# Attention with a feed-forward layer on one core: exponentials as the stationary operand of AV, two-bank QK units, and full tiles throughout

## The chip, the cores and the metric

The kernel runs on 1 core of one Trainium2 chip. The metric is the device time in microseconds (us) of one execution. Each time below is the median of several executions of the same kernel; where there was one execution only, the text says so. The profile is a recording of one such execution. Its engines are PE (matmuls), PEld (loading of the stationary operand, which may overlap PE), DVE (vector), ACT (activation functions), POOL and SP. PEclk is the clock that PE was granted, as a share of full speed.

## The reference

There are eight sequences (`t`) of 576 tokens with eight heads of 64. Attention has a bias that depends on the distance of the two tokens. Its output, 4608 tokens of 512, goes through a layer with a sine in it (called MoE in the code).

```python
scores = scale * np.matmul(q, k.transpose(0, 1, 3, 2)) + bias_table[bucket(|i - j|)]   # 8 x 8 x 576 x 576
attn = np.exp(scores - scores.max(-1)); attn = attn / attn.sum(-1)
x = np.matmul(attn, v)             # -> (4608, 512)
# ... 
h = x @ w_in                       # (4608, 2048)
s = np.sin(alpha * h)
g = h + s * s / (alpha + 1e-09)
out = g @ w_out                    # (4608, 512)
```

## The kernel before

The kernel makes a plan of tasks in advance and then writes out the instructions of each engine in the planned order. An engine carries out its instructions in that order. The waits between engines are not written by hand: the framework in which the kernel is written places them, from the tiles that each instruction reads and writes.

Heads are taken in pairs (`p`). The kernel computes transposed scores: keys lie on the partitions, queries along the row. A QK unit fills one bank of PSUM (the memory into which PE writes its results), ACT takes the exponential out of the bank into `u` (float16), and DVE multiplies the entries near the diagonal by the exponential of the bias (the band). AV then streams `u` past V as the weight, and once more past a block of ones, which gives the sum of each row in all 64 partitions of a head. The division is done as exp(-ln(sum)) on ACT and a multiplication on DVE.

```python
NBUF = {"sc": 4, "av": 2, "mo": 2, ...}        # PSUM: 8 banks of 128 x 512 float32

def new_sc():                                  # one score bank, four in rotation
    return ps.tile([128, 512], F32, name="sc", tag="sc", bufs=NBUF["sc"])

def mm2(out, lhsT, rhs, start, stop):          # two matmuls of 64 columns side by side
    for z in range(2):
        nc.tensor.matmul(out=out[64*z : 64*z+64], lhsT=lhsT[:, 64*z : 64*z+64], rhs=rhs, ...)

# a QK unit and its exponential: one bank (14 units per head pair)
def qk(e, ...):
    sc.v = new_sc()
    for y in range(nc_):
        for g in range(2):
            nc.tensor.matmul(out=sc.v[64*g : 64*g+64, n*y : n*y+n], lhsT=kzs[t%2][:, p, k0 : k0+64],
                             rhs=qTs[t%2][:, p, q0 : q0+n], start=True, stop=True)
def ex(e, ...):
    nc.scalar.activation(out=u.v[:, k0 : k0+nc_, q0 : q0+n], in_=sc.v[:, 0 : n*nc_], func=AF.Exp, scale=0.125)

# AV for a window of n queries (384, then 192): y = 0 gives the sums, y = 1 the values
def mm(e, y=y):
    o = avs[y].v = new_av()
    mm2(o[:, 0:n], (vhs[t%2][:, p] if y else ones2)..., u.v[:, 8, q0 : q0+n], True, False)
    for c in range(4):
        for z in range(2):
            nc.tensor.matmul(out=o[64*z : 64*z+64, 0:n],
                             lhsT=vs[t%2][:, c, 2*p+z, :] if y else ones,
                             rhs=u.v[:, 4*z+c, q0 : q0+n], ...)
# ACT: ln = Ln(sums); rd = Exp(-ln).   DVE: xT[:, p, ...] = avs[1] * rd
# ... 
# MoE-in for 512 tokens, f = 0..15; it uses the same four score banks
h.v = new_sc()
for j in range(4):
    mm2(h.v, w_in16[:, j, 128*f : 128*f+128], xT[:, j, ...512], j == 0, j == 3)
s16 = Sin(alpha * h)        # ACT
sq = s16 * s16              # ACT or DVE
g[:, f] = sq * inv_a + h    # DVE, reads h from the score bank again
# ... 
# MoE-out: 36 groups of 16 matmul pairs in the "mo" banks, used as filling for PE
```

In the steady part MoE-out of the previous tokens fills the gaps of PE during attention. ACT changes its function table twice per `t`, which marks the two phases in the trace: from the table of Exp to that of Sin is attention, from Sin to Exp is MoE-in.

The softmax here doesn't subtract the row's maximum and nothing guards it: scores larger than these inputs give would overflow.

## Time and profile before

The time is 446.31 us (three runs, 445.49 to 446.52).

| | before |
|---|---|
| span of the profiled run | 444.2 us |
| PE busy | 423.1 us, 95% |
| ACT busy | 382.9 us, 86% |
| second table load (end of the attention of t=0) | 50.0 us |
| attention + MoE-in, each t | 28.9 + 17.1 us |

The first fence is taken from the page of before: the busy time of each engine with the number of its instructions, and the busy tenths of PE and ACT and the granted clock in 40 equal slices.

```profile
span 444.2 us, 12031 instructions
PE 423.1 (95%) x4934; PEld 306.1 (69%) x4934; DVE 262.4 (59%) x554; ACT 382.9 (86%) x834; POOL 84.5 (19%) x95
...
PE   5579999999999999999999999999999999999996
...
ACT  3459999999999999999999999999999999946511
...
PEclk8659999999999999999999999999999999999999
```

From the fourth slice on PE is at 9 tenths or more at full clock, and so is ACT until the tail. A full PE with a full ACT beside it means that a gain has to come from PE, and that the plan has little slack.

The next fence has the groups of before that the change touches: instruction, its operands and count, then busy time and mean time of one, then how long the engine had been idle before them and what ended most of that.

```profile
L565 ACT ACTIVATE u<-sc 128x384 f16<-128x384 f32 x448 | 175.3, 527 | 7.6 <-PE sc L557 7.4
L377 PE MATMUL mo<-w_out,g 128*64 128x512 f16 x1152 | 172.2, 379 | 0.0
L557 PE MATMUL sc<-qT,kz 128*64 128x192 f16 (+1 forms) x1152 | 134.8, 296 | 8.8 <-DVE qT L470 5.3
L377 PE MATMUL sc<-xT,w_in 128*64 128x512 f16 x1152 | 132.7, 379 | 1.3 <-DVE g L708 1.3
```

The idle columns of the PE groups are what to read: 8.8 and 1.3 us in the whole run. PE hardly ever waits for a score bank. The mean time of a matmul (379 ns for 512 columns) holds its way through the array; what a matmul costs in a stream is the distance between two starts, which the timeline gives as 216 ns.

The view of the waits says the same for the stretch from 60 to 370 us. These are all its lines for PE: who waited for whom, total us, how often, and the longest.

```profile
PE sc L557 <- ACT u L565: 2.1, 5, 0.6
PE sc L377 <- DVE g L708: 0.5, 1, 0.5
```

The last view of before is one row of a table by stretches: length, busy us of each engine with its number of instructions, then granted clock, DMA share and GB/s.

```profile
core 0: us, PE busy (x) PEld busy (x) DVE busy (x) ACT busy (x) POOL busy (x), PEclk, DMA share, GB/s
...
144.00:188.00 44.00, 43.61 (x522) 32.62 (x520) 28.44 (x61) 43.03 (x97) 8.79 (x8) 1.00 0.91 107
```

### The profile page before, as it was taken

Reading aid. Unit: us, or ns where it says so; the run is one execution under the profiler, and the core shown is the slowest. Engines: PE = TensorE matmul, PEld = TensorE weight load, DVE = VectorE, ACT = ScalarE, POOL = GpSimd, SP = SyncE. Lnnn points to the kernel's source line nnn. Section 1 sums busy time; section 2 is a strip of 40 time slices with the busy share of each in tenths; the row PEclk is TensorE's granted clock in tenths of the full one; section 3 lists DMA queues with packets and bytes.
Section 4 is the critical chain, followed back from the end, with each engine's and each line's share of the span. In section 5 each row is a group of like instructions: output and inputs, shape, how many; then the busy total and the mean of one; then the engine's idle time right before and its main releaser. Section 6 shows DMA issues by size and latency. Waiting matters only on the chain.

```text
span 444.2 us, 12031 instructions
## 1 busy us (share of the span) xinstructions
PE 423.1 (95%) x4934; PEld 306.1 (69%) x4934; DVE 262.4 (59%) x554; ACT 382.9 (86%) x834; POOL 84.5 (19%) x95
## 2 busy tenths in 40 slices
PE   5579999999999999999999999999999999999996
PEld 3356657876688668865886688657876787666663
DVE  4447695549654865576456755685568545927400
ACT  3459999999999999999999999999999999946511
POOL 3792931016000700080008000400000000000000
PEclk8659999999999999999999999999999999999999
DMA  9999999939900996199209960980000000011111
GB/s 193 181 206 144 163 163 147 194 81 181 110 25 26 106 146 143 42 147 168 39 27 98 156 140 1 160 104 25 27 26 0 27 26 25 2 49 47 49 72 71
DMA packets 136118, 41.51 MB, mean 93 GB/s; under 512 B 122520, under 2 KB 130768, under 8 KB 136064
## 3 DMA queue, kind: packets, MB, share of 16 engines
q0 software_dynamic: 89392, 17.67, 47.3%
q1 hardware_dynamic: 46400, 22.79, 23.4%
q8 instruction: 38, 0.62, 0.6%
q10 hardware_dynamic: 272, 0.30, 0.2%
q14 instruction: 16, 0.13, 0.1%
HBM read 37.56 MB, written 16.52 MB: 122 GB/s over the span
## 4 chain that ended last, share of the span: by engine, by line
PE 71%; ACT 16%; issue 3%; DVE 3%; DMA 3%; POOL 2%; ACTq 0%; DVEq 0%; POOLq 0%
PE mo L377 24%; PE sc L377 18%; PE sc L557 14%; PE av L631 12%; ACT s L694 6%; ACT u L565 4%; PE av L377 3%; ACT L756 2%; ACT sq L701 2%; DVE g L708 1%; DMA w_out<-e_dram 1%; DMA tabL<-in_bias_table_dram 1%; DVE kz L470 1%; ACT rd L651 1%; ACT lnd L647 1%
## 5 line engine op out<-in xcount | busy, mean ns | idle before, releaser
L565 ACT ACTIVATE u<-sc 128x384 f16<-128x384 f32 x448 | 175.3, 527 | 7.6 <-PE sc L557 7.4
L377 PE MATMUL mo<-w_out,g 128*64 128x512 f16 x1152 | 172.2, 379 | 0.0
L557 PE MATMUL sc<-qT,kz 128*64 128x192 f16 (+1 forms) x1152 | 134.8, 296 | 8.8 <-DVE qT L470 5.3
L377 PE MATMUL sc<-xT,w_in 128*64 128x512 f16 x1152 | 132.7, 379 | 1.3 <-DVE g L708 1.3
L598 DVE TENSOR_TENSOR u<-u,m 128x512 f16<-128x512 f16 (+1 forms) x192 | 73.5, 400 | 72.1 <-ACT u L565 68.6
L557 PEld LDWEIGHTS <-kz 128*64 128x64 f16 x1152 | 84.7, 112 | 42.8 <-issue 10.6
L708 DVE SCALAR_TENSOR_TENSOR g<-sq,inv_a,sc 128x512 f16<-128x512 f16 x144 | 102.0, 745 | 20.6 <-PE mo L377 10.7
L377 PEld LDWEIGHTS <-w_in 128*64 128x64 f16 x1152 | 80.3, 110 | 44.1 <-issue 2.8
L694 ACT ACTIVATE s<-sc,alphaT 128x512 f16<-128x512 f32 x144 | 92.5, 678 | 3.5 <-PE sc L377 2.5
L377 PEld LDWEIGHTS <-g 128*64 128x64 f16 x1152 | 79.1, 110 | 22.5
L329 POOL DMA_DIRECT2D v<-in_v_dram x24 | 22.3, 1065 | 176.3 <-PE av L631 176.3
L701 ACT ACTIVATE sq<-s 128x512 f16<-128x512 f16 x75 | 47.2, 629 | 2.3
L662 DVE TENSOR_TENSOR xT<-av,rd 128x384 f16<-128x384 f32 (+1 forms) x68 | 29.4, 437 | 32.9 <-ACT rd L651 24.8
L631 PE MATMUL av<-u,ones 128*64 128x192 f16 (+1 forms) x512 | 44.8, 291 | 0.0
L631 PE MATMUL av<-u,v 128*64 128x192 f16 (+1 forms) x512 | 44.7, 291 | 0.0
L703 DVE TENSOR_TENSOR sq<-s 128x512 f16<-128x512 f16 x69 | 28.9, 420 | 11.4 <-ACT s L694 11.1
L647 ACT ACTIVATE lnd<-av 128x384 f32<-128x384 f32 x64 | 28.9, 451 | 7.3 <-PE av L631 6.5
L468 ACT ACTIVATE outs<-mo 128x512 f32<-128x512 f32 x15 | 8.9, 595 | 29.3 <-PE mo L377 29.3
L631 PEld LDWEIGHTS <-ones 128*64 128x64 f16 x512 | 30.8, 112 | 5.0
L631 PEld LDWEIGHTS <-v 128*64 128x64 f16 x512 | 30.7, 112 | 3.9
L651 ACT ACTIVATE rd<-lnd 128x384 f32<-128x384 f32 x64 | 28.7, 449 | 1.4
L377 PE MATMUL av<-u,ones 128*64 128x192 f16 (+1 forms) x128 | 20.5, 291 | 2.7 <-DVE u L581 2.7
(59 smaller groups left out, 194.0 us busy)
## 6 DMA issues: line engine op xcount, KB each, us to landing
out_dram<-outs SPq DMA_DIRECT2D x36, 256.0 KB, 2.0
staged_k<-in_k_dram POOLq DMA_DIRECT2D x6, 576.0 KB, 13.6
staged_q<-in_q_dram POOLq DMA_DIRECT2D x6, 576.0 KB, 16.7
kz<-kraw SPq DMA_DIRECT2D x12, 288.0 KB, 6.3
v<-in_v_dram POOLq DMA_DIRECT2D x24, 128.0 KB, 5.4
w_out<-in_v_dram SPq DMA_DIRECT2D x8, 256.0 KB, 5.4
w_in<-in_moe_w_in_dram POOLq DMA_DIRECT2D x4, 512.0 KB, 8.8
w_out<-in_moe_w_out_dram POOLq DMA_DIRECT2D x4, 512.0 KB, 8.8
```

The lines of the kernel that those rows point to most:

```text
L377: nc.tensor.matmul(out=out[64 * z : 64 * z + 64], lhsT=lhsT[:, 64 * z : 64 * z + 64], rhs=rhs, start=start, stop=stop,)
L557: nc.tensor.matmul(out=sc.v[64 * g : 64 * g + 64, n * y : n * y + n], lhsT=kzs[t % 2][:, p, k0 : k0 + 64], rhs=qTs[t % 2][:, p, q0 : q0 + ...
L565: nc.scalar.activation(out=u.v[:, k0 : k0 + nc_, q0 : q0 + n], in_=sc.v[:, 0 : n * nc_], func=AF.Exp, scale=0.125,)
L598: nc.vector.tensor_tensor(out=io, in0=io, in1=m2[:, 2 * p : 2 * p + 2, x0 : x0 + hi - lo], op=ALU.mult,)
L631: nc.tensor.matmul(out=o[64 * z : 64 * z + 64, 0:n], lhsT=vs[t % 2][:, c, 2 * p + z, :] if y else ones, rhs=u.v[:, 4 * z + c, q0 : q0 + n] ...
L647: nc.scalar.activation(out=ln.v[:, 0:n], in_=avs[0].v[:, 0:n], func=AF.Ln)
L651: nc.scalar.activation(out=rd.v[:, 0:n], in_=ln.v[:, 0:n], func=AF.Exp, scale=-1.0)
L662: nc.vector.tensor_tensor(out=xT[:, p, (x0 + a) % XN : (x0 + a) % XN + m - a], in0=avs[1].v[:, a:m], in1=rd.v[:, a:m], op=ALU.mult,)
L694: nc.scalar.activation(out=s16.v, in_=h.v, func=AF.Sin, scale=alphaT[:, f : f + 1])
L701: nc.scalar.activation(out=sq.v, in_=s16.v, func=AF.Square)
L703: k_of(e).tensor_tensor(out=sq.v, in0=s16.v, in1=s16.v, op=ALU.mult)
L708: nc.vector.scalar_tensor_tensor(out=gcell[b].v[:, f, :], in0=sq.v, scalar=inv_a[:, f : f + 1], in1=h.v, op0=ALU.mult, op1=ALU.add,)
```

## The change

The intent is to take streaming time from PE and work from ACT.

- In AV, `u` becomes the stationary operand: 128 queries by 128 keys is a weight, and V with a column of ones (65 columns) streams past it. The sums come out as one column beside the values, so the second pass over `u` goes. The output has queries on the partitions; it is normalised per row (reciprocal and multiply on DVE), turned by a transpose on PE and copied to `xT`. Ln and Exp(-Ln) on ACT go.
- QK fills two banks at a time, and one exponential of up to 768 columns reads both: 7 in place of 14 for each head pair.
- All matmuls use the whole array (128 columns of weights) instead of two halves.
- The bands read a reversed table with a negative step, so that the table no longer has to be turned on POOL. Loads and copies at the start are reordered.

```diff
-    def new_sc():
-        return ps.tile([128, 512], F32, name="sc", tag="sc", bufs=NBUF["sc"])
+    scb = ps.tile([128, 4, 512], F32, name="sc")
+    banks = [0]
+
+    def new_sc(n):
+        b = banks[0] % 4
+        banks[0] += n
+        return scb[:, b : b + n, :] if n > 1 else scb[:, b, :]
 ...
+    m2 = m2r[:, :, ::-1]
 ...
-    def mm2(out, lhsT, rhs, start, stop):
+    def full(out, lhsT, rhs, start, stop):
+        nc.tensor.matmul(out=out, lhsT=lhsT, rhs=rhs, start=start, stop=stop)
 ...
+                sc.v = new_sc(2)
+                for z in range(2):
+                        full(sc.v[:, z, n * y : n * y + n], kz[:, p, k0 : k0 + 128],
+                             qT[:, p, q0 : q0 + n], True, True)
 ...
+                    o, x = uz[:, :, c, 0:384], sc.v[:, :, 0:384]
+                nc.scalar.activation(out=o, in_=x, func=AF.Exp, scale=0.125)
 ... (AV: for each group of 128 queries at qc)
+                full(av.v[:, x0 : x0 + 2 * VC], u.v[:, 8, qc : qc + 128], vhs[t % 2][:, p, :],
+                     True, False)
+                for z in range(2):
+                    for c in range(4):
+                        full(av.v[:, x0 + VC * z : x0 + VC * z + VC],
+                             u.v[:, 4 * z + c, qc : qc + 128], vs[t % 2][:, c, 2 * p + z, :],
+                             False, z == 1 and c == 3)
 ...
+            nc.vector.reciprocal(out=r, in_=a[:, :, :, D])
+            nc.vector.tensor_tensor(out=xn..., in0=a[:, :, :, 0:D], in1=r..., op=ALU.mult)
 ...
+                nc.tensor.transpose(out=tr.v[:, qc - q0 : qc - q0 + 128], in_=xn.v[:, i], identity=id_sb)
 ...
-            def lg(e): ... func=AF.Ln
-            def rc(e): ... func=AF.Exp, scale=-1.0
```

## The prediction

> **What bounds the kernel now.** By the page's busy table PE is busy 95% of 444.2 us and ACT 86%; the slices show both at 9 tenths from about 45 us to 395 us. Table loads cut the span into iterations of 45.9 us (attention 28.9, MoE-in about 17). By the timeline, pairs of 64-column matmuls start every 216 ns for N=512, 162 ns for N=384 and 82 ns for N=192. Per iteration that makes 13.8 (MoE-in) + 13.8 (MoE-out) + 8.8 (QK) + 9.8 (AV with ones) = 46.2 us: PE streams without gaps and is the bound, with MoE-out filling the attention phase. ACT is nearly as full (about 45 us). The first 50 us (attention of t=0) are different: PE has only about 20 us of work there, much of it at half clock, and waits for loads, band tables and exponentials. After 373 us PE works alone.
>
> **What changes.**
> 1. AV per head pair: 20 paired streams (2.45 us) become 5 groups of one N=130 and eight N=65 matmuls, with u as a 128-column weight, plus 5 transposes of N=128. The question is whether a 128-column weight load hides behind 27 ns of streaming. The Trainium skill (TensorE: Matmul & The Clock Gate, Weight-path perf modes) says that fast weight load is on for 128 weights that are not fp32. The trace agrees as far as it goes: the first transposes (128-column weight, N=96) start every 42 ns at full clock, which is their streaming time; below 42 ns nothing is shown. My estimate is 31 ns per N=65: 5 x (8 x 31 + 57) + 5 x 56 = 1.8 us, so 0.65 us saved per pair, 2.6 us per iteration. At 42 ns almost nothing would be left (2.25 us).
> 2. QK, MoE-in and MoE-out as full tiles: a pair already streams as fast as one matmul, so no PE time is saved; only half the instructions go.
> 3. ACT loses Ln and Exp(-Ln) (1.41 us per pair from start to start, 45 us in all), and 14 exponentials become 7 (51 ns fixed each, 11 us in all); it gains some 30 copies to xT (about 11 us). Net about -45 us, but PE is the bound, so this is mostly off the critical path except in t=0.
> 4. DVE: the normalising multiply stays (reciprocal added, about 0.15 us), copies to xT are added, about +25 us in all. It was 59% busy: no bound. Bands now read a reversed table; the skill (Vector Engine (DVE) Microarchitecture Reference, Performance modes) lists steps of +-1 as fit for the two-per-cycle mode, so I expect the 128x512 band to stay near 0.44 us; no trace here shows it yet.
> 5. POOL loses the four table reversals (about 0.8 us each) and copies; the first pairs no longer wait for them. With shorter ACT work, t=0 attention should end near 42 us rather than 50.
>
> **Sum.** t=1..7: 7 x 2.6 = 18 us, all on the PE-bound path; start: about 8 us. 446.3 - 26 = **420 us**, range 407 to 435. Faster by over 2%: 0.88; within 2%: 0.10; slower: 0.02.
>
> **What would show it.** N=65 matmuls start every 29 to 34 ns; iterations shrink to 43 us or so; ACT falls to about 335 us busy with gaps in attention; DVE rises to about 290; PE without idle in t=1..7; second table load near 42 us.
>
> **What would make it wrong.** Weight loads of 128 columns that do not hide (42 ns or more per N=65); only two QK units in flight (two banks each of four), so that PE waits in order for ACT; the longer chain AV, reciprocal, multiply, transpose, copy delaying MoE-in beyond what MoE-out can fill; bands falling to one element per cycle; start-up loads arriving no earlier than before.

## The result, and the profile after

The changed kernel is correct and takes 827.11 us (four runs, 825.65 to 828.23) against 446.41 us of before in the same rounds. All four runs are alike, with a mean granted clock of 0.743 to 0.757. The ratio is 1.853, with a 95% interval of 1.850 to 1.856.

The page of after, the same lines as above:

```profile
span 823.8 us, 8773 instructions
PE 545.9 (66%) x3518; PEld 255.2 (31%) x3518; DVE 302.2 (37%) x683; ACT 357.1 (43%) x502; POOL 77.9 (9%) x88
...
PE   4665577656775678556765677557855777555588
...
ACT  2663256424642356225642365226542465222231
...
PEclk9995599857985599658975599559985699555569
```

No engine is full. The instructions went as intended (8773 in place of 12031) and so did ACT's work, yet PE is busy 66% and the clock falls to half over and over. Where every engine is idle a good part of the time, the engines wait for each other. The groups show between whom:

```profile
L391 PE MATMUL sc<-xT,w_in 128*128 128x512 f16 x576 | 238.0, 561 | 181.9 <-DVE g L716 130.9
L702 ACT ACTIVATE s<-sc,alphaT 128x512 f16<-128x512 f32 x144 | 98.9, 687 | 305.3 <-PE sc L391 183.0
...
L582 ACT ACTIVATE u<-sc 128x768 f16<-128x768 f32 (+1 forms) x224 | 171.0, 786 | 119.2 <-PE sc L391 112.4
...
L391 PE MATMUL sc<-qT,kz 128*128 128x192 f16 (+1 forms) x512 | 90.7, 293 | 60.3 <-ACT u L582 47.2
```

PE stood 181.9 us before MoE-in matmuls, against 1.3 us before the change; ACT stood 305.3 us before the sine, and what ended that was mostly PE. That is a ring: PE waits for the readers of the banks, and these wait for PE. The view of the waits has one line that betrays more:

```profile
PE sc L391 <- DVE g L716: 136.6, 69, 2.7
ACT s L702 <- DVE g L716: 122.4, 64, 2.5
...
PE sc L391 <- ACT u L582: 70.6, 115, 1.6
...
PE sc L391 <- ACT s L702: 53.6, 66, 1.7
```

The second line: ACT's sine waits for DVE's `g`, 122.4 us in all. Both only read the bank, and the `g` in question belongs to another `f`, in another bank. No data passes from one to the other. The chain of waits of after, between 253 and 261 us (start, length, what), shows a full turn:

```profile
253.62 1.88 PE sc L391 x4
...
255.51 0.69 ACT s L702
...
256.25 1.88 PE sc L391 x4
...
258.21 0.76 DVE g L716
...
258.99 0.70 ACT s L702
...
259.71 0.76 DVE g L716
...
260.51 1.88 PE sc L391 x4
```

For two `f` there are two matmul groups, two sines and two `g`, strictly one after the other: 6.9 us. PE's part is 3.76 us of that, and at half clock at that: each matmul of 512 columns takes 427 ns here and 216 ns in before. Attention has the same picture. This is the timeline of after (start, length, instructions, and in brackets the idle time before and what ended it):

```profile
292.80 0.81 ACT L582 ACTIVATE u<-sc 128x768 f16<-128x768 f32 x1 [0.57 <-PE sc L391]
...
293.66 0.48 PE L391 MATMUL sc<-qT,kz 128*128 128x384 f16 x2 [0.47 <-ACT u L582]
...
294.18 0.81 ACT L582 ACTIVATE u<-sc 128x768 f16<-128x768 f32 x1 [0.57 <-PE sc L391]
...
295.04 0.40 PE L391 MATMUL sc<-qT,kt 128*128 128x288 f16 x2 [0.68 <-ACT u L582]
```

QK starts 0.05 us after the exponential has ended (292.80 + 0.81 = 293.61), the exponential after QK has ended. There are four banks and a unit needs two, yet one unit is in flight. The row by stretches that answers to the one shown of before:

```profile
144.00:188.00 44.00, 25.90 (x92) 9.02 (x90) 12.91 (x24) 14.84 (x22) 9.23 (x8) 0.65 1.01 89
```

One t now takes about 91 us (36.9 to 39.8 of attention and some 52 of MoE-in), against 46.

### The profile page after: what moved, and what is told of

The parts are those of the page before. It is cut to its first block, busy times and chain, and to the rows that moved or that the text cites. A ratio compares the mean times of both kernels' runs of the same rounds, so it can differ in the third digit from the quotient of the medians.

```text
span 823.8 us, 8773 instructions
## 1 busy us (share of the span) xinstructions
PE 545.9 (66%) x3518; PEld 255.2 (31%) x3518; DVE 302.2 (37%) x683; ACT 357.1 (43%) x502; POOL 77.9 (9%) x88
## 4 chain that ended last, share of the span: by engine, by line
PE 54%; ACT 27%; DVE 14%; issue 3%; DMA 1%; DVEq 0%; ACTq 0%
PE sc L391 40%; ACT u L582 15%; DVE g L716 12%; ACT s L702 12%; PE mo L391 9%; PE av L391 4%; DMA e_dram<-e_sb 1%; DMA phi_sb<-phi_const 1%; DVE xn L653 1%; PE av L663 0%; DVE kt L518 0%; DVE rd L652 0%; DVEq L716 0%; DVE kz L472 0%; DVE qT L472 0%
## 5 line engine op out<-in xcount | busy, mean ns | idle before, releaser
L391 PE MATMUL sc<-xT,w_in 128*128 128x512 f16 x576 | 238.0, 561 | 181.9 <-DVE g L716 130.9
L702 ACT ACTIVATE s<-sc,alphaT 128x512 f16<-128x512 f32 x144 | 98.9, 687 | 305.3 <-PE sc L391 183.0
L582 ACT ACTIVATE u<-sc 128x768 f16<-128x768 f32 (+1 forms) x224 | 171.0, 786 | 119.2 <-PE sc L391 112.4
L391 PEld LDWEIGHTS <-w_in 128*128 128x128 f16 x576 | 72.9, 127 | 338.3 <-issue 325.0
L391 PE MATMUL mo<-w_out,g 128*128 128x512 f16 x576 | 175.2, 415 | 0.0
L391 PE MATMUL sc<-qT,kz 128*128 128x192 f16 (+1 forms) x512 | 90.7, 293 | 60.3 <-ACT u L582 47.2
L610 DVE TENSOR_TENSOR u<-u,m2r 128x512 f16<-128x512 f16 (+1 forms) x192 | 72.0, 390 | 42.7 <-ACT u L582 39.9
L391 PEld LDWEIGHTS <-g 128*128 128x128 f16 x576 | 60.2, 105 | 59.9 <-issue 24.3
L391 PEld LDWEIGHTS <-kz 128*128 128x128 f16 x512 | 46.7, 99 | 95.1 <-issue 85.1
L391 PEld LDWEIGHTS <-u 128*128 128x128 f16 x1440 | 57.3, 98 | 8.9
L391 PE MATMUL av<-v,u 128*128 128x65 f16 x1280 | 55.6, 194 | 0.0
```

What stands on the lines that cost most here:

```text
L391: nc.tensor.matmul(out=out, lhsT=lhsT, rhs=rhs, start=start, stop=stop)
L582: nc.scalar.activation(out=o, in_=x, func=AF.Exp, scale=0.125)
L610: nc.vector.tensor_tensor(out=io, in0=io, in1=m2[:, 2 * p : 2 * p + 2, x0 : x0 + hi - lo], op=ALU.mult,)
L702: nc.scalar.activation(out=s16.v, in_=h.v, func=AF.Sin, scale=alphaT[:, f : f + 1])
```

## The experiments

**The theory.** The four score banks are one tile in the change. The framework keeps track of accesses by tile, not by bank, and so every access to a bank waits for the last access of another engine to any of the four. The built program bears this out: the QK unit that fills banks 0 and 1 waits until ACT has finished its 69th counted instruction, which is the exponential of banks 2 and 3; the exponential of banks 0 and 1 is the 68th. This is so throughout: in the program rebuilt from the kernel of after, all 135 waits of a QK unit for an exponential name one of the other two banks, and 128 of the 144 sines wait for a `g` of another bank (in e1 none does). **Rivals:** (B) the lost clock is the cause and the waits follow from it; (C) two units of two banks are too few for any hardware, however the waits are placed.

Experiments with three rounds have intervals; those with one run are meant for effects of tens of per cent.

### e1: only the waits

Nothing of the work, the banks or the order on any engine is changed. A helper tells the framework, for each access, that there is no dependency between different banks, and adds those within a bank by hand.

```diff
+    def free_banks(i, used, write):
+        # keep the waits between accesses of one bank, drop those between banks
+        for x, bx, wx in sc_log[-48:]:
+            if not (used & bx) and x.engine != i.engine:
+                tc.declare_no_dep(i, x, reason="other bank")
+        ...  # the last accesses of the same bank: tc.add_manual_dep(i, x.name, ...)
-                        full(sc.v[:, z, 0:288], ...)
+                        free_banks(full(sc.v[:, z, 0:288], ...), {min(sc.b) + z}, True)
```

> The changed kernel with every instruction and its order on each engine kept; only the waits between accesses of DIFFERENT banks of the one four-bank score tile are dropped (waits between accesses of one bank are declared by hand). Theory A (because the four score banks are one tile, each access waits for the last access of any of the four banks, so one unit is in flight instead of two and four): 405 to 435 us, granted clock back to about 0.97, attention about 27 us and MoE-in about 17 us per iteration. Rival B (the low clock is the cause: full tiles, N=65 matmuls or transposes do not keep the clock granted, waits are its result): clock stays near 0.75 and the time above 650 us. Rival C (what my prediction named: two units in flight are too few for ACT and PE): attention stays near 37 us, the time above 520 us.

Measured: 425.22 us (424.84 to 425.53), ratio to before 0.953 [0.951, 0.955], 25.9 + 18.1 us for each t, correct; no race was found in the built program. The same stretch, then the timeline of e1 at the start of an attention phase:

```profile
144.00:188.00 44.00, 44.00 (x407) 25.39 (x404) 32.15 (x77) 39.21 (x58) 9.24 (x8) 1.00 0.98 107
```

```profile
293.30 3.74 ACT L609 ACTIVATE u<-sc 128x768 f16<-128x768 f32 x5
```

PE is busy 44.00 of 44 us at full clock, and five exponentials run without a gap where after had about 0.57 us before each. The order of the instructions is the same as in after on every engine, so the waits alone account for 827.1 - 425.2 = 402 us. Rival C falls: two units of two banks are enough. Rival B falls as the first cause: the clock came back without being touched.

### e2: the same one line in the kernel before

If the tile is the cause, it must ruin the kernel before as well, with none of the rest of the change.

```diff
     def new_sc():
-        return ps.tile([128, 512], F32, name="sc", tag="sc", bufs=NBUF["sc"])
+        b = banks[0] % 4
+        banks[0] += 1
+        return scb[:, b, :]          # scb = ps.tile([128, 4, 512], F32, name="sc")
```

> The kernel before with one edit: its four one-bank score tiles are cut from one four-bank tile, as in the changed kernel; column-tiled matmuls, Ln and one-bank units stay. Theory A: units go one by one, about 1.0 us per exponential unit (QK 0.16, hand-over about 0.4, exponential 0.49), 56 units per iteration, MoE-in near 50 us: 800 to 1000 us, clock below 0.9. Rivals B (full tiles or transposes lower the clock) and C (units of two banks): within 2% of 446 us.

Measured: 912.59 us (one run), clock 0.781, one t about 101 us. The line is enough: alone it doubles the time of the kernel before. That it is worse than the whole change fits the theory, since the single unit in flight is one bank here and two banks there.

### e3: four tiles, one exponential per bank

The ordinary way to have the banks apart: one tile per bank. An exponential can't span two tiles, so there are 14 again.

```diff
+    def one_sc():
+        return ps.tile([128, 512], F32, name="sc", tag="sc", bufs=NBUF["sc"])
     def new_sc(n):
-        b = banks[0] % 4 ...
+        return [one_sc() for _ in range(n)] if n > 1 else one_sc()
 ...
-                nc.scalar.activation(out=o, in_=x, func=AF.Exp, scale=0.125)
+                for z in range(2):   # o, x of bank z
+                    nc.scalar.activation(out=o, in_=x, func=AF.Exp, scale=0.125)
```

> The changed kernel with four one-bank score tiles; each QK unit takes two of them and its exponential becomes two instructions (14 per pair instead of 7). AV, transposes, full tiles, order of the plan unchanged. Theory A: 408 to 440 us, some 0 to 8 us over the kernel with only the cross-bank waits dropped, because ACT has 51 ns more per extra exponential, 11 us in all, mostly hidden. Rival B: clock near 0.75, above 650 us.

Measured: 422.33 us (421.97 to 422.90), ratio 0.946 [0.944, 0.948]; 25.4 + 18.1 = 43.5 us for each t. It does the work of the change apart from the two-bank exponentials, and it is 2.9 us faster than e1, where 0 to 8 us more had been expected. So no gain from the two-bank exponentials shows here: ACT is at about 40.5 of 44 us in the steady stretches of e3, where PE is at 44.00, and is not the bound. Why e1 is slower by that much was not tested; in e1 part of PE's waits sit on the weight loads (21.6 us in all), which hold up the stream behind them. That is an argument, not a finding.

### e4: two tiles of two banks

This keeps the two-bank exponential and separates the two units. In MoE-in two `f` still share a tile.

```diff
-    scb = ps.tile([128, 4, 512], F32, name="sc")
+    scb = [ps.tile([128, 2, 512], F32, name=f"sc{i}") for i in range(2)]
 ...
-        return scb[:, b : b + n, :] if n > 1 else scb[:, b, :]
+        return scb[b // 2] if n > 1 else scb[b // 2][:, b % 2, :]
```

> The changed kernel with the four score banks in two tiles of two banks instead of one of four; a QK unit is a whole tile, MoE-in still uses single banks. Theory A: attention recovers fully (about 27 us: two units in flight, as the plan meant), MoE-in stays slower than 17 us because neighbours share a tile (25 to 35 us): 470 to 600 us in all. Rival C: attention stays near 37 us.

Measured: 482.58 us (one run), clock 0.989; attention 25.6 us and MoE-in 25.4 us. Attention, where two units are in flight, is as good as with four tiles. MoE-in, where four banks were apart before, is 7.3 us longer than in e3, and PE stands for 5.3 us of it. The loss follows the number of separate tiles in each phase, as the theory has it.

### e5: filling the waits of MoE-in

This separates the lost clock from the waits. Every MoE-in group of after is followed by four idle matmuls into another bank, so that PE is kept busy; the waits stay.

```diff
+                if f == 0:
+                    idle[0] = new_av()
+                for j in range(4):
+                    full(idle[0], w_in16[:, j, 0:128],
+                         xT[:, j, 512 * b % XN : 512 * b % XN + 512], True, True)
```

> The changed kernel (one four-bank score tile, all its waits) with four extra matmuls of N=512 after each MoE-in group, on the same operands, into a spare bank that nobody reads: PE work put into time in which PE only waits. It splits the loss of 380 us into clock and waits. Theory A (the waits are the cause and the half clock in MoE-in follows from the idle PE): the clock in MoE-in returns to 1.0, each MoE-in group shrinks from 1.7 to 0.86 us, so MoE-in from about 52 to about 38 us per iteration: 690 to 740 us in all; the waits remain. If the clock alone were the cause (rival B): below 500 us. If idle PE does not set the clock: no gain, 827 us or more.

Measured: 737.81 us (one run), mean clock 0.995. The line of the clock in slices:

```profile
PEclk9899999999999999999999999999999999999999
```

The clock is back although every wait stays, so it had been lost to the idle time of PE. The half clock is worth about 827.1 - 737.8 = 89 us, and the waits at full clock about 737.8 - 425.2 = 313 us. The filling matmuls take some time of their own, so the first figure is rather too low than too high. MoE-in needs 43.0 us in e5 against some 52 in after (38 had been expected); attention is 37.7 us, within the range of after.

With the clock already at half, the gaps of PE in MoE-in of after are mostly 0.78 us and 2.0 to 2.4 us. Before the clock fell they were shorter. In the trace of after it fell at 242.4 us, for one:

```profile
240.71 1.02 PE L391 MATMUL sc<-xT,w_in 128*128 128x512 f16 x4 [1.52 <-ACT s L702]
243.29 1.86 PE L391 MATMUL sc<-xT,w_in 128*128 128x512 f16 x4 [1.56 <-DVE g L716]
```

The gap of 1.52 us is the longest in the 20 us before this fall; before the fall at 64.9 us it was 1.62 us, and before none of the other falls into a stage at half clock was it longer. The Trainium skill (TensorE: Matmul & The Clock Gate, "HAM oscillation") gives as its rule no gaps of PE of more than about 3.4 us; here the clock was lost with shorter ones. The next section of that page ("A second HAM failure mode: psum-queue depth-cycling") describes short idle times between matmul groups that do it, and this trace agrees with that one: granted clock 0.50 and PE busy 59 to 62% in four such stretches (157 to 195, 243 to 290, 335 to 375 and 423 to 471 us).

### e6 and e7: the first 46 us

In e3, the attention of t=0 ends at 46.2 us; 42 had been predicted. The timeline of ACT in e3 shows a wait of 5.5 us early on:

```profile
7.32 0.51 ACTq L441 DMA_DIRECT2D e_dram<-e_sb  x1
12.38 0.40 ACTq L403 DMA_DIRECT2D m2r<-e_dram  x1
12.82 0.65 ACT L468 ACTIVATE qT<-mo 128x576 f16<-128x576 f16 x1 [5.53 <-DMA e_dram<-e_sb]
14.03 1.64 ACT L580 ACTIVATE u<-sc 128x384 f16<-128x384 f32 x4 [0.57 <-PE sc L389]
```

The load of the band table is issued from ACT's own queue and has to wait for the store of that table; ACT's work behind it waits too. (The change moved this load to ACT; the first exponential of before was at 9.6 us.) e6 issues it from SP; e7 also lets the transposes of t=1 be planned later, since in e3 and e6 they stand in PE's order before their data is there (3.2 us in e6, once).

```diff
-    load_m2r(nc.scalar, 0, 2)      # e6
+    load_m2r(nc.sync, 0, 2)
-T_TR1 = 30.0                       # e7, added to e6
+T_TR1 = 42.0
```

> The kernel with four one-bank score tiles (422.3 us) with one edit: the first load of the band table is issued from the sync queue instead of from ACT, which in the trace of that kernel stands still from 7.3 to 12.8 us for the table's store to land before it may copy the first q. Theory (half of the missing start gain is this wait in ACT's order): first exponential at 10 us instead of 14 us, 417.5 to 421 us. Rival (the start is bound by the loads whatever the order): within 1 us of 422.3.

Measured: 422.80 us (422.33 to 423.04), ratio 0.949 [0.946, 0.951], so nothing against e3: a miss. The first exponential came at 12.9 instead of 14.0 us and the second table load at 44.1 instead of 46.2 us; PE then stood for the loads of t=1.

> As the run before it, and the transposes of the second sequence are planned at 42 instead of 30 us, so that PE and ACT do not wait in order for their loads (gaps of 3.3 and 3.0 us at 41 and 50 us in the trace) in the middle of the first sequence. Theory: 3 to 6 us less than the run before it: 412 to 418 us. Rival (the loads bound the start): no change to the run before it.

Measured: 415.99 us (415.12 to 416.57), ratio 0.933 [0.931, 0.936]. The second table load is at 38.5 us, the steady part as in e3. This is, with e9 below, the fastest version. An improvement at one place of the start showed only when the next wait in order was taken away as well.

### e8: back to 64-column matmuls, except in AV

The prediction said that full tiles save no PE time. This puts QK, MoE-in and MoE-out of e3 back to pairs of half tiles; AV stays as changed.

```diff
+    def pair(out, lhsT, rhs, start, stop):
+        for z in range(2):
+            nc.tensor.matmul(out=out[64*z : 64*z+64], lhsT=lhsT[:, 64*z : 64*z+64], rhs=rhs, ...)
-                        full(sc.v[z][:, ...], ...)        # likewise in MoE-in and MoE-out
+                        pair(sc.v[z][:, ...], ...)
```

> The kernel with four one-bank score tiles, with QK, MoE-in and MoE-out again as pairs of 64-column matmuls as in the kernel before, and only AV and transposes as full tiles. My claim that full tiles save no PE time by themselves: 420 to 426 us. Rival (going from column tiles to full tiles makes PE drain, so the AV change pays only with all full tiles): 224 changes and back per run; at 0.1 us each 45 us more, above 435 us.

Measured: 449.64 us (447.74 to 450.13), ratio 1.008 [1.005, 1.011]; 28.4 + 18.8 us for each t. The claim of the prediction falls. From the starts in the trace: where PE goes from a pair of half tiles to a full tile, the next start comes after 312 ns instead of 216 (512 columns); from AV (65 columns) to a half tile, after 123 instead of 29; from a transpose to a half tile, after 149 instead of 56. In the timeline of e8, and of e3 for comparison:

```profile
278.07 0.60 PE L393 MATMUL mo<-w_out,g 128*64 128x512 f16 x4
278.60 0.28 PE L668 MATMUL av<-id_sb,xn 128*128 128x128 f16 x2
278.81 0.41 PE L393 MATMUL mo<-w_out,g 128*64 128x512 f16 x2
```

```profile
297.22 0.81 PE L389 MATMUL mo<-w_out,g 128*128 128x512 f16 x3
297.87 0.33 PE L661 MATMUL av<-id_sb,xn 128*128 128x128 f16 x3
```

In e3 three full tiles take 0.65 us, 3 x 216 ns. In e8 two pairs take 0.53 us where 2 x 216 ns would be 0.43, and two transposes 0.21 us where 2 x 56 ns would be 0.11. That is about 95 ns for each change of form. The trace of e8 has 255 changes and that of e3 has 24, all at the start; the 231 more make about 22 of the 27.3 us by which e8 is slower than e3. The rest was not traced. The Trainium skill (TensorEngine Tiling (Array Packing), "Key Properties") says that changing the tiling mode drains the engine; it gives no figure, and this run supplies one.

So the new AV alone, among half tiles, gains nothing (449.6 against 445.5 us of before). It pays because everything else became a full tile with it.

### e9 and e10: two more at the fastest version

e9 puts the first cast on DVE ahead of the clearing of buffers. e10 plans each bank by itself, with one task for its QK and one for its exponential.

```diff
     nc.scalar.dma_start(out=e_dram.ap(), in_=e_sb)
-    clear(nc.vector, 0)            # e9
     cast0(0, nc.vector)
+    clear(nc.vector, 0)
 ...
-            b, sc = [Buf("sc"), Buf("sc")], Cell()      # e10, added to e9
+            for z in range(2):
+                b, sc = Buf("sc"), Cell()               # one QK task, one Exp task for each bank
```

> The run with the reordered start (416.0 us), with one more edit: DVE casts the first k before it clears the zero halves, instead of after. In the trace of that run the first q copy on ACT waits 4.4 us for PE's transposes, which wait 3.5 us for this cast. Theory: first exponential near 9.5 us instead of 12.2, MoE-in of the first sequence earlier by the same: 412 to 415.5 us. Rival (the loads of the band table and of the second pair bind next): within 1 us of 416.0.

Measured: 416.39 us (415.41 to 417.60), ratio 0.934 [0.932, 0.937], the same as e7: a miss. The first exponential came at 10.9 us, but ACT then stood 2.3 us at about 20 us, waiting for QK on PE. QK waited for a copy on DVE that stands behind a band, and DVE had been idle for 3.2 us before that band (in e7 for 2.3 us, put down there to the load of the band table).

> As the run before it, and the plan handles QK and exponentials bank by bank (a bank is free as soon as its own exponential is done; ACT's cost in the plan is that of two instructions). In the steady iterations PE idles below 0.2 us per iteration already and the period is 43.5 us, so theory (PE is the bound, ACT's granularity is off the path): the period stays within 0.3 us of 43.5, the total within 3 us of the run before it. Rival (ACT hand-over still costs): period 42.5 us or less, 8 us or more saved.

Measured: 419.56 us (418.51 to 419.99), ratio 0.940 [0.938, 0.942], which is 3.2 us slower than e9. The steady part did get shorter (about 43.0 us for each t), but the tail from the last table load to the end grew from 61.4 to 72.1 us: less MoE-out had been used as filling, and PE did it alone at the end (182 of its 576 matmuls after the last table load, 133 in e9). Both theory (43.5 us within 0.3, total within 3 us) and rival (42.5 us or less, 8 us saved) missed, the theory by little. An iteration that is shorter because filling was put off is no gain.

## Why the prediction was wrong, and where it was right

The prediction was 420 us, with a chance of 0.02 for slower; 827 us came.

**The step that failed** is the one in "What would show it": "PE without idle in t=1..7". It rested on an assumption that was not checked, that at least two QK units would be in flight. The prediction even named the danger as "only two QK units in flight (two banks each of four)", and the truth was below that: one. The four score banks had become one tile, and each access waited for the last access to any bank by another engine, even read after read. With it PE stood some 29 us of 91 in each t (8.7 in attention, about 20.6 in MoE-in). By the runs the waits themselves cost about 313 us and the half clock that followed about 89 us. e1 (same instructions, same order, other waits: 425.2 us), e2 (one tile in the kernel before: 912.6 us) and e4 (two tiles: attention healed, MoE-in not) show this. The line of the diff and the order of instructions were both in view before the run; what was not looked at was which instruction each wait of the built program points to.

**Term by term, with the waits mended (e1, e3):**

1. *AV at about 31 ns for each matmul of 65 columns.* Right. The trace of after, slowed as it was, already shows it: the timeline below has one group of 128 queries (one matmul of 130 columns, eight of 65) from 296.73 to 297.03 us, 0.30 us; less 56 ns for the first, that is about 30 ns each. The median distance of starts is 29 ns, the mean in e3 32 ns. The weight of 128 columns hides behind 65 columns of streaming. The Trainium skill (TensorE: Matmul & The Clock Gate, "Weight-path perf modes") says that the fast weight load is on for 128 weights that are not fp32. The distance of 29 ns fits that; the mode itself is not visible in a trace. The record of a single such load is about 98 ns long, so it overlaps several matmuls.

```profile
296.73 0.22 PE L391 MATMUL av<-vh,u 128*128 128x130 f16 x1
296.78 0.41 PE L391 MATMUL av<-v,u 128*128 128x65 f16 x8
297.03 0.22 PE L391 MATMUL av<-vh,u 128*128 128x130 f16 x1
```

2. *2.6 us less for each t, 18 us for t=1..7.* Right in size: 45.9 to 43.5 us in e3, which is 2.4 us, and from the second table load to the end 394.2 to 374.9 us, 19.3 us saved. The sum fits better than its parts, and that is partly luck: of the 19.3 us, only 9.2 lie between the second and the last table load, where the first iteration even became 3.9 us longer; the other 10.1 are in the tail, since PE had done more of MoE-out as filling (after the last table load 133 matmuls of it were left, against 366 halves, that is 183 pairs, in before). And the reason given for item 2 of the prediction was incomplete. *"A pair already streams as fast as one matmul, so no PE time is saved"* holds only in a kernel without other forms. With the new AV among half tiles, each change of form costs about 95 ns (e8), and the gain of AV is gone.
3. *ACT at about 335 us busy.* e1 has 338.3. That the 14 exponentials became 7 was put down as ACT's gain, and rightly as off the critical path: e3 has 14 again, 347.4 us, and is no slower.
4. *DVE at about 290 us; a band of 128x512 near 0.44 us with a negative step.* e1 has 291.2, and the band took 423 ns on average there, 422 in after (442 before). The Trainium skill (Vector Engine (DVE) Microarchitecture Reference, section 5.1) lists a step of plus or minus 1 for the two-per-cycle mode; the run agrees for one negative source.
5. *The start, 8 us sooner, second table load near 42 us.* Wrong in size: 3.8 us (46.2 us in e3). The cause is the load of the band table on ACT's queue together with the transposes of t=1 in PE's order. With both mended (e7) the load came at 38.5 us, and the kernel ended at 416.0 us, inside the range that had been given and below its middle.

Of the dangers that the prediction named, weight loads that do not hide and bands that fall to one element per cycle did not happen, and the longer chain behind AV did not hold PE up (in e3 PE waits 1.9 us in all for `xn`). Starting loads that come no earlier happened in part (term 5).

**What stays open.** Why e1 is 2.9 us slower than e3 was only argued. Full tiles in all places with the AV of before were not run, so what they would give alone is not known. What share of idle time makes the clock fall is not known beyond the two cases here.

## What to carry to other kernels

When buffers that used to be separate become slices of one tile, look at which earlier instruction each wait of the built program points to: a wait between two readers, or between different banks, is the sign, and no count of instructions or of engine time shows it. When no engine is full after a change, look for the ring in the chain of waits before looking at the costs of the operations. Keep the form of the matmuls the same across the streams that interleave on PE, since a cheap new stream can be eaten by the changes of form that it brings.

## What the Trainium skill lacked or had wrong

- No page has it: a tile that spans several PSUM banks can be guarded as one thing by a framework, whichever bank is meant. PSUM — Partial Sum Buffer gives the rule to guard by bank and quadrant, but not that warning. The runs: 827.1 us with one tile of four banks, 482.6 with two tiles, 422.3 with four; and 912.6 against 446 us for the kernel before.
- TensorE: Matmul & The Clock Gate, "HAM oscillation": the rule against gaps over about 3.4 us is too weak. In after the clock fell to 0.5 with no gap over 1.62 us in the 20 us before, and stayed there with gaps of mostly 0.78 to 2.4 us and PE busy 59 to 62%. The section after it describes such cases, without any figure for how much idle time is too much.
- TensorE: Matmul & The Clock Gate, "Back-to-back issue gap": about 81 ns at N=128 and 131 ns at N=512 are given for sustained pairs of weight load and matmul. With a new 128-column weight for each, the runs show 56 ns (N=128) and 216 ns (N=512), and 29 ns at N=65.
- TensorEngine Tiling (Array Packing), "Key Properties": no figure for the drain at a change of mode. e8 shows about 95 ns for each change between 64-column and 128-column matmuls; 231 changes more than in e3 make about 22 of the 27.3 us between the two.
- Vector Engine (DVE) Microarchitecture Reference, section 5.1: the negative step is named as not measured. A multiply of two float16 sources, one with a negative step, took 422 ns for 128x512, against 442 ns with positive steps.
